# Two large writes of staged rows, moved on the ScalarE queue out of the step that ends a block

## The chip, the cores and the metric

One core of one Trainium2 chip runs the whole program. The metric is the device time of one execution in microseconds (us), as the median of the runs shown. A profiled execution of its own gives the trace; times in it are counted from the start of its span.

## The reference, cut to what matters

A long convolution (by FFT, over 12480 positions, 128 channels, batch 2) is gated by its input and goes through two dense layers:

```
h_filt = (maximum(pos_emb @ w1, 0) @ w2) * window
y = irfft(rfft(x * v, n=L) * rfft(h_filt, n=L), n=L)[:, :S]    # L = 2 * S
x = (x * y).reshape(B * S, 128)
h = x @ w_in1;  x = (h * clip(h + 3, 0, 6) / 6) @ w_out1       # 128 -> 2048 -> 128
h = maximum(x @ w_in2, 0);  out = (h * h) @ w_out2
```

## The kernel before

The program has three stages. The first (to about 64 us) makes the filter. The second, the convolution, is a loop of steps `i`, 0 to 97, written out by hand; every engine runs its instructions in the order of the program, and this order is what the change touches. The third (from about 490 us) takes 64 tiles of 390 tokens through the dense layers.

The convolution works on 32 groups of four channels, three items to a group: item 3g is the filter, 3g+1 and 3g+2 are the two batch entries. In step `i` item `i+3` gets its first transform (`s1`, TensorE line 178, eight matmuls), then `twiddle` on VectorE (lines 188 to 194, the last sum on GpSimd for filter items). Item `i+2` is rounded to a high part by ScalarE (`split1`, tile `h`, line 202); GpSimd subtracts that to make the low part (tile `l`, line 203). Item `i` gets its second transform (`s2`, line 217, twelve matmuls of which the first two need `h` and the next two `l`). Then come `filt` (ScalarE, lines 224 to 226) for a filter item, or `prod` (lines 236 to 241, VectorE and GpSimd) for a batch item. Item `z = i-2`, if it is a batch item, gets its inverse transform (`s3`, line 248) and is copied by ScalarE (`keep`, line 257) into a tile of staged rows, `stg`. So a step whose `z` is a filter item (`z % 3 == 0`, that is `i % 3 == 2`) has neither `s3` nor `keep`.

A block is four groups, twelve steps. When the last item of a block is kept, in step 12b+13 for block b, ScalarE itself issues the DMAs that write the 128 staged rows to memory: two of 4 rows (`zda`) and two of 60 rows (`zdb`, 1350 KB each), in `write`, line 360. There are two `stg` tiles, used in turn. The last block, 7, is finished apart: its large rows are written from SyncE's queue after the loop. SyncE also issues the loads of `x` and `v` (lines 149, 150), nine items ahead; GpSimd multiplies them (`product`, line 155).

Of the kernel before, what the change touches and what calls it, by code (L numbers as in the profile page):

```python
# [30 lines left out]
ZA = 4  # L31
# [8 lines left out]
def tile_hyena_moe(ctx: ExitStack, tc, xg, vg, xT, pos, w1d, w2d, win, fmat, twc,  # L40
                   tws, dcs, inv, vtab, w_in1, w_out1, w_in2, w_out2, out):
    nc = tc.nc
# [6 lines left out]
    zds = [tc.dram_tile([2, ZA, NBLK, K1, 64], F32, name="zda"),  # L49
           tc.dram_tile([2, 64 - ZA, NBLK, K1, 64], F32, name="zdb")]  # L50
# [95 lines left out]
    def load(g, b):  # L146
        xt = xv.tile([N1, 4, 128], F32, name=f"x{g}_{b}", tag="x", bufs=3)
        vt = xv.tile([N1, 4, 128], F32, name=f"v{g}_{b}", tag="v", bufs=5)
        nc.sync.dma_start(xt, xg[g, b])
        nc.sync.dma_start(vt, vg[g, b])  # L150
        us[(g, b)] = (xt, vt)

    def product(g, b):
        xt, vt = us[(g, b)]
        nc.gpsimd.tensor_tensor(vt, vt, xt, ALU.mult)
        us[(g, b)] = vt
# [11 lines left out]
    def s1(i, pool=None):  # L168
        g, s = divmod(i, 3)
        ps = bank(f"p1_{i}", pool)  # L170
        for c in range(4):
            if s == 0:
                ch = 4 * g + c
                src = hs[ch // 32][:N1, ch % 32, :]
            else:
                src = us[(g, s - 1)][:, c, :]
            o = 256 * (c % 2)
            nc.tensor.matmul(ps[:, c // 2, o:o + 2 * K1], src, fm)  # L178
        ps1s[i] = ps

    def twiddle(i):
        pv = ps1s.pop(i).rearrange("p a (s f) -> p (a s) f", s=2)[:, :, :2 * K1]
        at = vp.tile([128, 4, 2, K1], F32, name=f"a1_{i}", tag="A", bufs=3)
        bt = vp.tile([128, 4, 2, K1], F32, name=f"b1_{i}", tag="B", bufs=3)
        cw, sw = (w.rearrange("p r k -> p (r k)").unsqueeze(1)
                   .to_broadcast([128, 4, 2 * K1]) for w in (cc, ss))
        av, bv = (t.rearrange("p s r k -> p s (r k)") for t in (at, bt))
        nc.vector.tensor_tensor(bv, pv, sw, ALU.mult)  # L188

        on_pool = i and i % 3 in SUM1_POOL  # L190
        first = av if on_pool else pv
        nc.vector.tensor_tensor(first, pv, cw, ALU.mult)  # L192
        eng = nc.gpsimd if on_pool else nc.vector
        eng.tensor_tensor(at, first.rearrange("p s (r k) -> p s r k", r=2),  # L194
                          bt[:, :, ::-1, :], ALU.add)
        g1[i] = at

    def split1(i):
        gt = g1.pop(i)
        h = vp.tile([128, 4, 2, K1], F32R, name=f"h1_{i}", tag="hi", bufs=3)  # L200
        l = vp.tile([128, 4, 2, K1], F32R, name=f"l1_{i}", tag="lo", bufs=3)
        nc.scalar.activation(h, gt, AF.Copy)  # L202
        nc.gpsimd.tensor_tensor(l, gt, h.bitcast(F32), ALU.subtract)  # L203
        hi1[i], lo1[i] = h, l

    def s2(i):
        ps = bank(f"p2_{i}")
        h, l = hi1.pop(i), lo1.pop(i)
        for o in range(2):

            pv = ps[:, o, :K4].rearrange("p (s k) -> p s k", s=4)
            terms = ((o, 0), (1 - o, 1 if o == 0 else 2))
            ops = [(dcl[:, m], h[:, :, r, :]) for r, m in terms]
            ops += [(dch[:, m], l[:, :, r, :]) for r, m in terms]
            ops += [(dch[:, m], h[:, :, r, :]) for r, m in terms]
            for n, (wt, x) in enumerate(ops):
                nc.tensor.matmul(pv, wt, x, start=(n == 0), stop=(n == len(ops) - 1))  # L217
        ps2s[i] = ps

    def filt(i):  # L220
        ps = ps2s.pop(i)
        hr = vp.tile([128, K4], F32, name=f"hr_{i}", tag="hr", bufs=1)
        h2 = vp.tile([128, 2, K4], F32, name=f"hq_{i}", tag="h2", bufs=1)
        nc.scalar.activation(hr, ps[:, 0, :K4], AF.Copy)
        nc.scalar.activation(h2[:, 0], ps[:, 1, :K4], AF.Copy)
        nc.scalar.activation(h2[:, 1], ps[:, 1, :K4], AF.Copy, scale=-1.0)
        hh[i // 3] = (hr, h2)

    def prod(i):
        ps = ps2s.pop(i)  # L230
        hr, h2 = hh[i // 3]
        pv = ps[:, :, :K4]
        at = vp.tile([128, 2, K4], F32, name=f"a2_{i}", tag="Y", bufs=3)
        bt = vp.tile([128, 2, K4], F32, name=f"b2_{i}", tag="B", bufs=3)
        on_pool = i % 3 in SUM2_POOL
        nc.vector.tensor_tensor(bt, pv, h2, ALU.mult)
        first = at if on_pool else pv
        nc.vector.tensor_tensor(first, pv, hr.unsqueeze(1).to_broadcast([128, 2, K4]),
                                ALU.mult)
        eng = nc.gpsimd if on_pool else nc.vector  # L240
        eng.tensor_tensor(at, first, bt[:, ::-1, :], ALU.add)
        y2[i] = at

    def s3(i):
        y = y2.pop(i)
        ps = bank(f"p3_{i}")
        for r in range(2):
            nc.tensor.matmul(ps[:, r, :K4], iv[:, r], y[:, r])  # L248
        ps3s[i] = ps

    def keep(i):
        g, s = divmod(i, 3)
        blk, ch0 = g // 4, (g % 4) * 4
        ps = ps3s.pop(i)
        if blk not in stg:
            stg[blk] = sp.tile([128, K1, 2, 2, 16], F32, name=f"stg{blk}", tag="stg")
        nc.scalar.activation(
            stg[blk][:, :, :, s - 1, ch0:ch0 + 4].rearrange("p k r c -> p r c k"),
            ps[:, :, :K4].rearrange("p r (c k) -> p r c k", c=4), AF.Copy)
        if g % 4 == 3 and s == 2:  # L260
            sv = stg.pop(blk).rearrange("p k r b c -> p k (r b c)")
            if blk == NBLK - 1:

                for h, t in enumerate((za, zb)):
                    nc.scalar.dma_start(t.rearrange("k d r b c -> k d (r b c)")[:, blk], sv[64 * h:64 * h + 1])
                tail.append(sv)
            write(blk, 0, sv)
            if blk < NBLK - 1:
                write(blk, 1, sv)


    with tc.tile_pool(name="mlp", bufs=2, side="right") as mp, \
# [83 lines left out]
    with tc.tile_pool(name="cv_ps", bufs=4, space=PSUM) as vps:  # L356
        def write(blk, z, sv, queue=nc.scalar):
            lo, hi = ((0, ZA), (ZA, 64))[z]
            for h in range(2):
                queue.dma_start(zds[z][h, :, blk], sv[64 * h + lo:64 * h + hi])  # L360

        tail = []
        s1(0)
        twiddle(0)
        s2(1)
        s1(3)
        split1(0)
        twiddle(3)
        s2(2)
        product(1, 0)  # L370
        product(1, 1)
        load(2, 0)
        load(2, 1)
        for i in range(NI + 2):

            a, z = i + AH, i - 2
            if i < NI and i not in (1, 2):
                s2(i)
            if 3 < a < NI:
                s1(a)  # L380
            if 0 <= z < NI and z % 3:
                s3(z)
            if 2 < a - 1 < NI:
                split1(a - 1)
            if 0 <= i < NI:
                if i % 3 == 0:
                    filt(i)
                else:
                    prod(i)
            if 3 < a < NI:  # L390
                twiddle(a)
            if 0 <= z < NI and z % 3:
                keep(z)
            if i == 27:
                raw_weight(1)

            for t, f in ((a + 6, load), (a + 3, product)):
                g, s = divmod(t, 3)
                if s and (2 if f is load else 1) < g < G:
                    f(g, s - 1)  # L400
            if i == NI - 1:

                room = hp.tile([128, 2, 3, FF // 4], F32, tag="h2", name="room")
                room0 = hp.tile([128, 7, 512], F32, tag="h3", name="room0")
                other = parts[(1, 3)] = decoding(None, 1, 3, nc.gpsimd)
                for _ in range(5):
                    next(other)
                decode(None, 1, 0)
                next(other)
                next(other)  # L410
                parts[(1, 1)] = decoding(None, 1, 1)
                for _ in range(5):
                    next(parts[(1, 1)])
                za, zb = (room0[:K1, k].rearrange("k (d r b c) -> k d r b c", d=NBLK, r=2, b=2) for k in (0, 1))
                vt = {0: room0[:K1, 2, :4 * N1].rearrange("k (q r n) -> k q r n", q=2, r=2)}
                xt = {0: room0[:, 3, :TOK]}
                tile_loads(0, za, zb, vt[0], xt[0])
# [313 lines left out]
```

## Time and profile before

| | before |
|---|---|
| median of 3 runs | 2869.82 us (2868.83 to 2870.09) |
| the profiled execution's own time | 2869.38 us |
| its span in the trace | 2867.6 us |
| granted TensorE clock, mean | 0.991 of 2.4 GHz |
| TensorE busy: matmul, weight load | 2779.6 us, 2711.9 us |
| VectorE, ScalarE, GpSimd busy | 2122.8, 2006.1, 1570.8 us |

The span runs from the first instruction to the last; 1.8 us of the execution lie outside it. DMA-issuing instructions stand in the trace, on the queue of the engine that issues them (`ACTq`, `SPq`), but are not counted as busy time of the engine. Matmuls overlap each other, so that a busy TensorE is not one at its peak; the weight loads (`PEld`) show its waits more closely.

### The profile page before, as it was taken

The page shows a single profiled execution, that of the slowest core. Times are in us where ns is not written, and L with a number is a line of the kernel's source. Part 1 is how long each engine was busy: PE and PEld are TensorE (multiplying, and loading weights), DVE is VectorE, ACT ScalarE, POOL GpSimd, SP SyncE. Part 2 cuts the span into 40 slices and gives each one's busy share as a digit, 9 for nine tenths or more (in the row PEclk, how much of TensorE's full clock was granted, in tenths as well). Part 3 has the DMA queues.
Part 4 walks back from the last instruction along what each step waited for, and adds up shares of the span by engine and source line. Part 5 has one row for each costly group of instructions (what it writes and reads, how often), then busy time and mean ns, then how long its engine had stood idle before and what let it go on. Part 6 is the DMA issues. An engine that isn't in the chain of part 4 may idle for free.

```text
span 2867.6 us, 42099 instructions
## 1 busy us (share of the span) xinstructions
PE 2779.6 (97%) x15712; PEld 2711.9 (95%) x15712; DVE 2122.8 (74%) x2280; ACT 2006.1 (70%) x2630; POOL 1570.8 (55%) x1020
## 2 busy tenths in 40 slices
PE   7999998888999999999999999999999999999999
PEld 5888887778999999999999999999999999999999
DVE  6888888899877777777777777777777777777666
ACT  6445445666777777777777777777777777777776
POOL 4888885655455555555555555555555555554444
PEclk9999999999999999999999999999999999999999
DMA  4343433321011111111110111111111111110000
GB/s 158 103 137 106 140 108 88 101 60 30 24 27 26 26 26 27 26 26 26 26 27 24 26 26 27 26 26 26 26 26 26 26 26 27 26 26 6 10 12 15
DMA packets 139419, 125.77 MB, mean 44 GB/s; under 512 B 99692, under 2 KB 122702, under 8 KB 137806
## 3 DMA queue, kind: packets, MB, share of 16 engines
q1 hardware_dynamic: 128322, 89.23, 11.4%
q10 hardware_dynamic: 10892, 33.86, 4.0%
q8 instruction: 123, 2.02, 0.3%
q14 instruction: 82, 0.67, 0.1%
HBM read 86.64 MB, written 36.37 MB: 43 GB/s over the span
## 4 chain that ended last, share of the span: by engine, by line
PE 83%; DVE 7%; issue 5%; ACT 2%; POOL 2%; DMA 0%; POOLq 0%; ACTq 0%; DVEq 0%
PE acc L561 36%; PE ph L515 36%; PE p L217 4%; PE py L459 3%; PE p L178 2%; PE p L248 1%; DVE g L531 1%; ACT h L331 1%; DVE a L194 1%; POOL l L203 1%; DVE b L188 1%; DVE p L192 1%; DVE wa L106 1%; DVE wa L104 0%; DVE gl L544 0%
## 5 line engine op out<-in xcount | busy, mean ns | idle before, releaser
L544 POOL TENSOR_TENSOR gl<-g,gh 128x780 fp32r<-128x780 f32 x522 | 984.2, 1885 | 1156.1 <-ACT gh L541 1151.5
L541 ACT ACTIVATE gh<-g 128x780 fp32r<-128x780 f32 x1024 | 869.1, 849 | 111.7 <-DVE g L531 61.9
L561 PE MATMUL acc<-gh,wp 128*128 128x390 f32 x4096 | 922.4, 347 | 6.3 <-DVE wp L119 6.3
L531 DVE SCALAR_TENSOR_TENSOR g<-r,ph 128x780 f32<-128x780 f32 x512 | 494.2, 966 | 350.8 <-POOL gl L544 285.8
L561 PEld LDWEIGHTS acc<-gh,wp 128*128 128x128 f32 x4096 | 729.6, 189 | 6.6 <-issue 6.6
L534 DVE SCALAR_TENSOR_TENSOR g<-ph,r 128x780 f32<-128x780 f32 x512 | 496.4, 970 | 277.8 <-POOL gl L544 244.1
L522 ACT ACTIVATE r<-ph,three 128x780 f32<-128x780 f32 x512 | 467.5, 913 | 254.5 <-PE ph L515 239.9
L515 PE MATMUL ph<-oh,wp 128*128 128x390 f32 x2048 | 635.7, 351 | 5.5 <-DVE g L531 4.2
L515 PE MATMUL ph<-xh,wp 128*128 128x390 f32 x2048 | 618.7, 343 | 0.0
L524 ACT ACTIVATE r<-ph 128x780 f32<-128x780 f32 x512 | 422.4, 825 | 235.8 <-PE ph L515 233.8
L561 PE MATMUL acc<-gl,wp 128*128 128x390 f32 x2048 | 537.9, 344 | 21.4 <-POOL gl L544 18.9
L544 DVE TENSOR_TENSOR gl<-g,gh 128x780 fp32r<-128x780 f32 x502 | 501.2, 998 | 0.6
L561 PEld LDWEIGHTS acc<-gl,wp 128*128 128x128 f32 x2048 | 372.9, 189 | 33.2 <-POOL gl L544 23.3
L515 PEld LDWEIGHTS ph<-oh,wp 128*128 128x128 f32 x2048 | 385.4, 191 | 7.7 <-DVE g L531 6.1
L515 PEld LDWEIGHTS ph<-xh,wp 128*128 128x128 f32 x2048 | 381.4, 189 | 0.0
L515 PE MATMUL ph<-ol,wp 128*128 128x390 f32 x1024 | 350.5, 342 | 0.0
L515 PE MATMUL ph<-xl,wp 128*128 128x390 f32 x1024 | 348.4, 340 | 0.0
L202 ACT ACTIVATE h<-a 128x720 fp32r<-128x720 f32 x96 | 76.7, 806 | 221.5 <-DVE a L194 133.8
L203 POOL TENSOR_TENSOR l<-a,h 128x720 fp32r<-128x720 f32 x96 | 168.0, 1750 | 94.1 <-ACT h L202 94.1
L515 PEld LDWEIGHTS ph<-ol,wp 128*128 128x128 f32 x1024 | 194.8, 190 | 0.3 <-DVE ol L475 0.3
L515 PEld LDWEIGHTS ph<-xl,wp 128*128 128x128 f32 x1024 | 192.6, 188 | 0.0
L447 POOL TENSOR_TENSOR pn<-za,zb 90x256 f32<-90x256 f32 x126 | 132.2, 1068 | 0.0
(90 smaller groups left out, 2711.0 us busy)
## 6 DMA issues: line engine op xcount, KB each, us to landing
zdb<-stg ACTq DMA_DIRECT2D x14, 1350.0 KB
x<-xg SPq DMA_DIRECT2D x64, 196.0 KB
v<-vg SPq DMA_DIRECT2D x64, 196.0 KB
out<-ot ACTq DMA_DIRECT2D x64, 195.0 KB
xt<-xT SPq DMA_DIRECT2D x63, 195.0 KB
za<-zdb SPq DMA_DIRECT2D x60, 180.0 KB
zb<-zdb SPq DMA_DIRECT2D x60, 180.0 KB
vt<-vtab SPq DMA_DIRECT2D x63, 137.8 KB
```

What stands on the lines that cost most here:

```text
L203: nc.gpsimd.tensor_tensor(l, gt, h.bitcast(F32), ALU.subtract)
L217: nc.tensor.matmul(pv, wt, x, start=(n == 0), stop=(n == len(ops) - 1))
L447: nc.gpsimd.tensor_tensor(t[:, :, r], za[:, :, r], zb[:, :, 1 - r], op)
L459: nc.tensor.matmul(ps[:, o:o + n], pm[j][q][:, r, b, :], v[:, q, r, :n], start=(r == 0), stop=(r == 1))
L515: nc.tensor.matmul(ps[:, c, :TOK], wt, x, start=(m == 0), stop=(m == 2))
L522: nc.scalar.activation(r, ph[n][:, :, :TOK], AF.Relu, bias=three)
L524: nc.scalar.activation(r, ph[n][:, :, :TOK], AF.Relu)
L531: nc.vector.scalar_tensor_tensor(g, r, 6.0, pv, ALU.min, ALU.mult)
L534: nc.vector.scalar_tensor_tensor(g, pv, 0.0, r, ALU.max, ALU.mult)
L541: nc.scalar.activation(h, g, AF.Copy)
L544: eng.tensor_tensor(l, g, h.bitcast(F32), ALU.subtract)
L561: nc.tensor.matmul(ps, wt, x, start=(q == 0 and m == 0), stop=(q == NP - 1 and m == len(ops) - 1))
```

## The change

For blocks 0 to 6 the two writes of 60 rows no longer follow the writes of 4 rows. They go into a list, and each of the next two steps without a `keep` issues one of them from ScalarE: steps 12b+14 and 12b+17.

```
             write(blk, 0, sv)
             if blk < NBLK - 1:
-                write(blk, 1, sv)
+
+                late_rows.extend((blk, h, sv) for h in range(2))
...
-        tail = []
+        tail, late_rows = [], []
...
             if 0 <= z < NI and z % 3:
                 keep(z)
+            elif late_rows:
+                blk, h, sv = late_rows.pop(0)
+                nc.scalar.dma_start(zds[1][h, :, blk], sv[64 * h + ZA:64 * h + 64])
```

ScalarE's instructions at the end of block 2, from the last copy of the block on, before. The first number in a name is the item; `stg2` is the block's tile, and what stands in brackets is what an instruction waits for (`DMAHW` are the counters that tell of a DMA's landing).

```order
L257 ACTIVATE stg2_1741<-p3_35_2105 128x2x4x90 [waits PE_49]
L360 DMA zda_65<-stg2_1741 4x5760 [waits DMAHW3_49,Activation_49]
L360 DMA zda_65<-stg2_1741 4x5760 [waits DMAHW5_49]
L360 DMA zdb_66<-stg2_1741 60x5760 [waits DMAHW6_49]
L360 DMA zdb_66<-stg2_1741 60x5760 [waits DMAHW7_49]
L202 ACTIVATE h1_40_2150<-a1_40_2117 128x720 [waits DVE_49]
L202 ACTIVATE h1_41_2190<-a1_41_2159 128x720 [waits DVE_49,PE_49]
```

The same place now:

```order
L257 ACTIVATE stg2_1740<-p3_35_2105 128x2x4x90 [waits PE_49]
L361 DMA zda_65<-stg2_1740 4x5760 [waits DMAHW3_49,Activation_49]
L361 DMA zda_65<-stg2_1740 4x5760 [waits DMAHW5_49]
L202 ACTIVATE h1_40_2148<-a1_40_2117 128x720 [waits DVE_49]
L397 DMA zdb_66<-stg2_1740 60x5760 [waits DMAHW6_49]
L202 ACTIVATE h1_41_2189<-a1_41_2157 128x720 [waits DVE_49,PE_49]
L224 ACTIVATE hr_39_2193<-p2_39_2168 128x360 [waits PE_49]
```

The high part of item 40 has moved ahead of both writes of 60 rows; one of them stands between items 40 and 41, the other has left the place.

Three steps later on ScalarE, before:

```order
L202 ACTIVATE h1_42_2227<-a1_42_2199 128x720 [waits Pool_49]
L257 ACTIVATE stg3_2204<-p3_38_2224 128x2x4x90 [waits PE_49]
L202 ACTIVATE h1_43_2265<-a1_43_2236 128x720 [waits DVE_49,Activation_49]
L202 ACTIVATE h1_44_2305<-a1_44_2274 128x720 [waits DVE_49,PE_49,Activation_49]
L224 ACTIVATE hr_42_2309<-p2_42_2284 128x360 [waits PE_49,Activation_49]
```

The same place now:

```order
L202 ACTIVATE h1_42_2226<-a1_42_2198 128x720 [waits Pool_49]
L257 ACTIVATE stg3_2203<-p3_38_2223 128x2x4x90 [waits PE_49]
L202 ACTIVATE h1_43_2264<-a1_43_2235 128x720 [waits DVE_49,Activation_49]
L397 DMA zdb_66<-stg2_1740 60x5760 [waits DMAHW3_49]
L202 ACTIVATE h1_44_2305<-a1_44_2273 128x720 [waits DVE_49,PE_49,Activation_49]
```

The second write now stands between the high parts of items 43 and 44, where ScalarE had no DMA before. On the other four engines the order of the instructions is the same in both kernels.

## Rows read from the trace of the kernel before

**Rows 1.** The page: chain that ended last, share of the span by engine.

```profile
PE 83%; DVE 7%; issue 5%; ACT 2%; POOL 2%; DMA 0%; POOLq 0%; ACTq 0%; DVEq 0%
```

**Rows 2.** Windows, line 217 alone: stretch, length, busy (instructions), clock, DMA share, GB/s.

```profile
125.20:458.15 332.95, 181.56 (x900) 154.76 (x900) 0.98 0.43 128
198.75:235.44 36.69, 21.15 (x108) 18.30 (x109) 1.00 0.38 110
```

**Rows 3.** TensorE's timeline: start us, us, instruction, count, idle before and its end.

```profile
125.23 0.60 PE L217 MATMUL p<-h,dcl 128*128 128x360 f32 x1
...
198.77 0.46 PE L217 MATMUL p<-h,dcl 128*128 128x360 f32 x1
...
232.06 0.77 PE L217 MATMUL p<-h,dcl 128*128 128x360 f32 x2
...
235.46 0.63 PE L217 MATMUL p<-h,dcl 128*128 128x360 f32 x2
...
241.50 0.60 PE L217 MATMUL p<-h,dcl 128*128 128x360 f32 x2 [1.28 <-ACT h L202]
243.30 0.60 PE L217 MATMUL p<-l,dch 128*128 128x360 f32 x2 [1.21 <-POOL l L203]
...
247.25 0.60 PE L217 MATMUL p<-h,dcl 128*128 128x360 f32 x1
...
458.20 0.60 PE L217 MATMUL p<-h,dcl 128*128 128x360 f32 x1
```

**Rows 4.** Waits, 126 to 470 us: us in total, times, longest us.

```profile
POOL l L203 <- ACT h L202: 65.5, 49, 4.4
...
ACT h L202 <- DMA zda<-stg: 33.0, 5, 6.6
PEld p L217 <- ACT h L202: 13.4, 7, 2.1
PEld p L217 <- POOL l L203: 10.5, 7, 1.5
...
ACT h L202 <- DMA zdb<-stg: 6.9, 1, 6.9
...
ACT h L202 <- DVE b L188: 6.6, 1, 6.6
```

**Rows 5.** ScalarE's timeline around the end of block 2.

```profile
227.77 0.81 ACT L202 ACTIVATE h<-a 128x720 fp32r<-128x720 f32 x1 [4.55 <-DVE a L194]
...
229.19 0.47 ACT L226 ACTIVATE hq<-p 128x360 f32<-128x360 f32 x1
...
234.09 0.59 ACTq L360 DMA_DIRECT2D zda<-stg  x2
234.72 5.88 ACTq L360 DMA_DIRECT2D zdb<-stg  x2
240.64 1.50 ACT L202 ACTIVATE h<-a 128x720 fp32r<-128x720 f32 x2 [6.59 <-DMA zda<-stg]
```

**Rows 6.** GpSimd's timeline in the same stretch.

```profile
236.13 1.29 POOL L155 TENSOR_TENSOR v<-v,x 98x512 f32<-98x512 f32 x1
241.53 1.72 POOL L203 TENSOR_TENSOR l<-a,h 128x720 fp32r<-128x720 f32 x1 [4.11 <-ACT h L202]
```

**Rows 7.** Windows, all engines: PE, PEld, DVE, ACT, POOL busy, clock, DMA share.

```profile
188.00:195.30 7.30, 6.10 (x23) 5.48 (x24) 2.40 (x4) 3.90 (x6) 6.34 (x5) 0.77 0.96 307
241.50:247.20 5.70, 4.50 (x23) 3.88 (x24) 1.85 (x4) 3.07 (x5) 5.67 (x4) 1.00 0.90 297
238.30:250.50 12.20, 9.71 (x52) 8.15 (x51) 8.12 (x10) 6.79 (x9) 8.06 (x6) 1.00 0.87 254
```

**Rows 8.** Tile `stg`: count, duration in ns (least, median, most), first and last start.

```profile
L360 ACTq DMA_DIRECT2D zda<-stg x16: 246/301/513, 127.3 to 491.1; - x16
L360 ACTq DMA_DIRECT2D zdb<-stg x14: 2649/2913/3036, 128.1 to 446.7; - x14
...
L360 SPq DMA_DIRECT2D zdb<-stg x2: 397/432/468, 499.0 to 499.5; - x2
```

**Rows 9.** VectorE's timeline around the end of block 2.

```profile
230.17 0.91 DVE L236 TENSOR_TENSOR b<-p,hq 128x720 f32<-128x720 f32 x1 [0.89 <-PE p L217]
...
233.64 0.91 DVE L194 TENSOR_TENSOR a<-p,b 128x720 f32<-128x720 f32 x1
...
238.98 0.91 DVE L194 TENSOR_TENSOR a<-p,b 128x720 f32<-128x720 f32 x1
```

## The prediction

> **What bounds the kernel now.** I read the page's chain first: it lies on TensorE for 83% of the span [rows 1], so a change is worth what it takes out of TensorE's waits, or nothing. The change touches the convolution steps alone, so the next question is how long those take when nothing disturbs them. Line 217 runs twelve matmuls a step. Between 198.75 and 235.44 us, where no block ends, 108 of them (nine steps) take 36.69 us, or 12.23 us for three steps, at a granted clock of 1.00 [rows 2]. From 125.20 to 458.15 us, which begins just before the end of block 0 and closes just after that of block 6, 900 of them (75 steps, 25 times three) take 332.95 us [rows 2]; the first matmul of a step marks both ends [rows 3]. Undisturbed that would be 25 x 12.23 = 305.75 us. So **27.2 us** are lost there, and seven blocks end there.
>
> Where it goes is seen at the end of block 2. ScalarE issues the two small writes (0.59 us) and then the two large ones, and is held by these for 5.88 us; the next high part, of item 40, starts at 240.64, after 6.59 us in which ScalarE computes nothing [rows 5]. Its input was ready at 233.64 + 0.91 = 234.55 [rows 9]. GpSimd, which makes the low part from it, was done with its earlier work at 236.13 + 1.29 = 237.42 and stood for 4.11 us [rows 6]. TensorE ran dry for 1.28 us until the high part came and again for 1.21 us until the low part came [rows 3]. Step 41 starts at 247.25; step 38 had started at 232.06, and three undisturbed steps later is 244.29: 2.96 us lost [rows 3]. It is the same at all seven ends: ScalarE's high parts wait behind the DMA issues 5 + 1 times by name and once under VectorE's (33.0 + 6.9 + 6.6 = 46.5 us, 6.6 each), and the weight loads of line 217 wait seven times for the high and seven times for the low part, 13.4 + 10.5 = 23.9 us [rows 4].
>
> Seven times 2.96 is 20.7 us. The other 6.5 I put down to the clock: in 188.0 to 195.3, behind the end of block 1, the granted clock was 0.77 on average, between the two levels of 1.2 and 2.4 GHz, against 1.00 at the same place of block 2 (241.5 to 247.2) [rows 7]. In both TensorE had just waited; in the first it then ran slowly for a while.
>
> **The change part by part.**
>
> *Removed:* two issues of 2.65 to 3.04 us, median 2.91 [rows 8], from ahead of the high part. What is left ahead of it are the small writes, which end at 234.09 + 0.59 = 234.68, 0.13 us after the input is ready [rows 5, 9]. The high part then starts at about 234.7. GpSimd takes it up when its own queue allows, at 237.42, and needs 1.72 us: 239.14 [rows 6]. TensorE wants both at 241.50 - 1.28 = 240.22 [rows 3], 1.1 us later. So both waits go, and nothing else is late there: VectorE had finished the next sum, for item 41, at 239.89 during the stall [rows 9].
>
> *First half, one step later.* It stands between the high parts of items 40 and 41. ScalarE is free at 234.72 + 0.81 = 235.53 and is next wanted at 239.89, 4.36 us later; an issue at the median ends at 238.44, 1.45 us early, at the longest 1.32 us early. Cost nothing; the cover is ScalarE's wait for VectorE.
>
> *Second half, three steps on.* In an undisturbed group of three steps ScalarE waits 4.55 us for VectorE at this place [rows 5]. 2.91 us fit, with 1.6 to spare. Cost nothing, same cover.
>
> *Bounds of an issue alone.* The trace has no large write that is issued by itself on ScalarE. From below: the same shape took SyncE 0.40 and 0.47 us for block 7 [rows 8]; from above I take the whole pair, 5.88 us [rows 5], in case an issue lasts until something earlier has gone through. I take 2.91, the row of the same engine and tile; 0.4 gives the same time, since both hide. At 5.88 the high part is 1.3 (second half) to 1.5 us late. Queued behind it are the three copies of the filter, which end at 229.19 + 0.47 = 229.66; VectorE uses them at 230.17 [rows 5, 9], so 0.5 us of this is slack and at most 1.0 us remains. Fourteen times: 14 us given back.
>
> *The clock's 6.5 us.* From below 0 (the clock falls anyway), from above all of it. I take all: the low clock stands behind a wait that is gone.
>
> *Transfers, queues and buffers.* No bytes are added. The two large writes of a block now start 12 us apart; before, the DMA engines were at 0.87 of their time for the 12.2 us behind a block's end, against 0.38 undisturbed [rows 7, 2], so loads issued there have less in their way. SyncE, GpSimd, VectorE and TensorE keep their order. A staged tile is written again by the block after next, fourteen steps after its own block's end, and its second half leaves four steps after that end: ten steps, some 41 us, remain for the landing.
>
> Sum against the profiled execution: 2869.38 - 27.2 = 2842.2 us; the median of the runs lies 0.44 us above that execution, so **2842.6 us**. What follows step 89 is moved as a whole.
>
> **The rivals.**
>
> *A part comes back.* The issue lasts longer than the gap, or the clock falls without a wait. For it: the pair held ScalarE for 5.88 us, and nothing shows what it waited for. Against it: all fourteen lie between 2.65 and 3.04, whichever stood first [rows 8]. At the upper bound 14 us come back: 2856.6 us; with the clock's 6.5 alone 2849.1 us.
>
> *No change: transfers bind.* If the stall were the transfers' (0.87 of the engines' time), splitting them in time would gain nothing, since the bytes stay: 2869.8 us. For it: the DMA share. Against it: what TensorE waits for is a high part, which no DMA feeds, and GpSimd's only listed wait is for it too, 65.5 us [rows 4], none for a loaded tile. The Trainium skill ("DMA: Bandwidth & Descriptors", section "Issuing engines are not separate DMA queues") says that all issuing engines share the same 16 DMA engines, and that what is saved by where a DMA is initiated is the sequencer's time, usually small beside the transfer. By that rule the time would stay at 2869.8. The row disagrees on "small": 5.88 us on ScalarE's queue, with TensorE waiting behind it.
>
> *Slower: each issue holds ScalarE to the end of the traffic ahead of it.* There would then be fourteen stalls in place of seven. The place is the high part behind each write. It is covered by the gap (4.4 to 4.55 us) and by 0.5 us of slack, so it costs from an issue of about 5 us on; it eats the 27.2 us when each costs TensorE 1.94 us, at about 7 us, and is slower from there. The traffic behind a block's end lasts 12 us at 0.87 [rows 7]; an issue of 8 us would cost 14 x 3.0 = 42 us and give 2869.8 - 27.2 + 42 = 2884.6 us. Against it: 3.04 us is the longest in the trace, and in fourteen cases none lasted as long as the traffic.
>
> **How the numbers follow.** Forecast (2840 to 2847 us, some tenths of a microsecond left per block): 0.79. A part comes back (2847 to 2862): 0.12. No change: 0.05. Slower: 0.04. About 0.2%, or 5.7 us, can be told from no change. The range takes in the forecast and the greater part of the second case: 2839 to 2853 us, which leaves out less than 2 in 10. Faster: 0.79 + 0.12 = 0.91; same 0.05; slower 0.04.
>
> **What would show it.** Right: 900 matmuls of line 217 from the step behind block 0's end take 306 to 309 us; in that stretch the weight loads' waits for high and low parts are under 3 us; fourteen issues of at most 3 us, each followed by a high part that still waits for VectorE; a clock of 1.00 behind every block's end. Wrong: a high part that waits for a DMA issue, now fourteen times; GpSimd waiting for a load; a late product on VectorE behind the filter's copies; or the same 27 us turning up as a wait between step 89 and the first tile of the dense layers.

## The result and the profile after

The changed kernel takes 2842.7 us (median of 4 runs, 2840.06 to 2843.33) against 2869.32 us for the one before (4 runs beside them, 2868.39 to 2870.09): a ratio of 0.9906, 95% interval 0.9888 to 0.9923. The forecast was 2842.6 us. The profiled execution has a span of 2840.9 us where it was 2867.6.

The page's chain, share of the span by engine, against [rows 1]:

```profile
PE 89%; DVE 5%; issue 2%; ACT 2%; DMA 1%; POOL 1%; SPq 0%; ACTq 0%; POOLq 0%; DVEq 0%
```

Windows, line 217 alone, over the same 75 steps as the first of [rows 2] (stretch, length, busy and count, clock, DMA share, GB/s):

```profile
126.28:432.02 305.74, 176.30 (x900) 152.46 (x900) 1.00 0.48 134
```

The 900 matmuls take 305.74 us in place of 332.95: 27.2 us less, and as long as 75 undisturbed steps. The granted clock of the stretch is 1.00, where it was 0.98. Nothing else carries weight. The program ahead of the stretch took 1.08 us longer than in the profile before (its first matmul stood at 125.23 and stands at 126.31), though it is the same program, and what follows it took 2408.83 us instead of 2409.40: -27.2 + 1.1 - 0.6 gives the 26.7 us between the spans.

Waits of all engines from 126 to 432 us (us in total, times, longest us), against [rows 4]:

```profile
ACT h L202 <- DVE a L194: 128.5, 50, 4.6
POOL l L203 <- ACT h L202: 36.6, 50, 0.9
DVE b L236 <- PE p L217: 22.3, 25, 0.9
ACT h L202 <- POOL a L194: 21.9, 26, 0.9
PEld p L217 <- issue: 9.0, 25, 0.4
```

No high part waits for a DMA, and the weight loads' waits for high and low parts (13.4 and 10.5 us before) are not in the list. GpSimd's longest wait for a high part is 0.9 us, where it was 4.4.

ScalarE's timeline around the end of block 2, against [rows 5]:

```profile
226.16 0.59 ACTq L361 DMA_DIRECT2D zda<-stg  x2
226.81 0.80 ACT L202 ACTIVATE h<-a 128x720 fp32r<-128x720 f32 x1 [0.67 <-DVE a L194]
226.83 2.81 ACTq L397 DMA_DIRECT2D zdb<-stg  x1
232.07 0.81 ACT L202 ACTIVATE h<-a 128x720 fp32r<-128x720 f32 x1 [4.46 <-DVE a L194]
...
238.96 0.81 ACT L202 ACTIVATE h<-a 128x720 fp32r<-128x720 f32 x1 [0.61 <-DVE a L194]
238.98 0.32 ACTq L397 DMA_DIRECT2D zdb<-stg  x1
```

The high part of item 40 follows the small writes at once. The first large write is held for 2.81 us and is through at 229.64; the next high part starts at 232.07, when VectorE is ready for it. The second takes 0.32 us. Both begin 0.02 us after the high part ahead of them has begun, not when it ends.

GpSimd and TensorE at the same place, from their timelines, against [rows 6, 3]:

```profile
229.47 1.72 POOL L203 TENSOR_TENSOR l<-a,h 128x720 fp32r<-128x720 f32 x1
```

```profile
232.12 0.57 PE L217 MATMUL p<-h,dcl 128*128 128x360 f32 x2
232.53 0.50 PE L217 MATMUL p<-l,dch 128*128 128x360 f32 x2
...
236.38 0.77 PE L217 MATMUL p<-h,dcl 128*128 128x360 f32 x2
```

The low part is made at 231.19, 0.9 us before TensorE starts the step, and neither row of TensorE has a wait in brackets.

Windows behind the ends of blocks 1 and 2, all engines, at the places of [rows 7] in the program (the third is the 12.2 us behind block 2):

```profile
183.20:190.50 7.30, 7.30 (x42) 6.84 (x42) 6.21 (x8) 5.87 (x8) 5.88 (x5) 1.00 0.91 265
232.10:237.80 5.70, 5.70 (x32) 5.25 (x32) 4.82 (x6) 4.87 (x7) 4.26 (x4) 1.00 0.82 222
230.40:242.60 12.20, 12.20 (x70) 11.16 (x69) 11.05 (x14) 6.25 (x8) 10.76 (x8) 1.00 0.85 230
```

TensorE is busy throughout and the clock is 1.00 at both ends, where one was 0.77. The DMA engines are about as full behind block 2's end as before (0.85 against 0.87).

### The profile page after: what moved, and what is told of

Its sections match the earlier page's. It is cut to its first block, busy times and chain, and to the rows that moved or that the text cites. A ratio compares the mean times of both kernels' runs of the same rounds, so it can differ in the third digit from the quotient of the medians.

```text
span 2840.9 us, 42092 instructions
## 1 busy us (share of the span) xinstructions
PE 2771.1 (98%) x15712; PEld 2708.3 (95%) x15712; DVE 2122.7 (75%) x2280; ACT 2006.0 (71%) x2630; POOL 1570.6 (55%) x1020
## 3 DMA queue, kind: packets, MB, share of 16 engines
q1 hardware_dynamic: 128322, 89.23, 11.5%
## 4 chain that ended last, share of the span: by engine, by line
PE 89%; DVE 5%; issue 2%; ACT 2%; DMA 1%; POOL 1%; SPq 0%; ACTq 0%; POOLq 0%; DVEq 0%
PE acc L565 36%; PE ph L519 36%; PE p L217 7%; PE p L178 4%; PE py L463 3%; PE p L248 2%; DVE g L535 1%; DMA zdb<-stg 1%; DVE wa L106 1%; ACT h L332 1%; DVE wa L104 0%; DVE gl L548 0%; POOL gl L548 0%; ACT gh L545 0%; DVE wa L100 0%
```

## The experiments

All seven are edits of the changed kernel or of the one before. A median is that of four executions; the ratio is to executions of the kernel before beside them. "Loss" is the length of the 75 steps of line 217 (900 matmuls in all) above 305.75 us, from the same view as above, in the profiled execution. The kernel before has 27.2 and the changed one 0.0.

| kernel | median us | ratio to before, 95% interval | loss us |
|---|---|---|---|
| first half early | 2844.47 | 0.9922 (0.9907 to 0.9936) | 3.4 |
| both in the next step | 2852.05 | 0.9944 (0.9929 to 0.9959) | 8.5 |
| large first, small moved | 2842.86 | 0.9912 (0.9895 to 0.9928) | 0.1 |
| both four steps later | 2842.98 | 0.9913 (0.9899 to 0.9928) | 0.0 |
| order swapped, none moved | 2855.32 | 0.9952 (0.9937 to 0.9967) | 10.5 |
| small writes from SyncE | 2900.44 | 1.0112 (1.0095 to 1.0129) | 48.6 |
| both in the next step, weight later | 2845.11 | 0.9919 (0.9904 to 0.9933) | 2.2 |

**First half early.** One large write goes back ahead of the high part.

```
             write(blk, 0, sv)
             if blk < NBLK - 1:
-                late_rows.extend((blk, h, sv) for h in range(2))
+                nc.scalar.dma_start(zds[1][0, :, blk], sv[ZA:64])
+                late_rows.append((blk, 1, sv))
```

> The first large write of a block goes back behind the two small ones, ahead of item 40's high part; the second stays one step later. Theory (an issue is held only while two DMAs issued before it still stand in the queue; what costs is how late the high part gets): the issue is held about 2.8 us, the high part starts about 3 us late, GpSimd makes the low part from about 238.4 to 240.1 on the clock of the kernel before, and TensorE wants it at 240.2, so at most 0.3 us a block is lost: 2842 to 2845 us, and the second write, alone, is issued in about 0.3 us. Rival (each large write ahead of a high part costs half of the stall): 13.6 us of the 27.2 come back, 2856 us.

2844.47 us, as the theory had it (the profiled execution was the slowest of the four, 2849.03 us). A high part that starts 2.9 us late costs nothing at the block's end: TensorE has no wait there at any of the seven ends, and the four steps behind an end are no more than 0.02 us longer than in the changed kernel. So half of the stall is not half of the loss. The 3.4 us stand six and seven steps further on, 0.1 to 0.9 us at five of the first six blocks and 1.7 at block 3. There GpSimd's product waits 0.95 to 2.6 us for a load of `x` or `v`, which it does nowhere in this stretch of the changed kernel; why these loads land later is open. All engines behind the end of block 3 and twenty us on, then the wait between:

```profile
278.00:292.00 14.00, 14.00 (x82) 12.96 (x80) 12.61 (x16) 7.16 (x10) 11.86 (x9) 1.00 0.74 207
296.50:305.50 9.00, 8.32 (x46) 7.27 (x45) 7.37 (x9) 5.46 (x8) 5.72 (x4) 1.00 0.31 94
```

```profile
POOL v L155 <- DMA v<-vg: 2.6, 1, 2.6
```

The second issue did not come as expected: tile `stg` shows both large writes held.

```profile
L269 ACTq DMA_DIRECT2D zdb<-stg x7: 2667/2842/2843, 131.0 to 427.6; - x7
L397 ACTq DMA_DIRECT2D zdb<-stg x7: 2672/2967/2985, 133.7 to 430.8; - x7
```

I had counted the second one as alone. ScalarE issues it 0.07 us after the first is through, since the high part between them does not hold the queue (at block 6 alone 0.36 us after); so it is the fourth of one group, as before the change.

**Both in the next step.**

```
             elif late_rows:
-                blk, h, sv = late_rows.pop(0)
-                nc.scalar.dma_start(zds[1][h, :, blk], sv[64 * h + ZA:64 * h + 64])
+                for blk, h, sv in late_rows:
+                    nc.scalar.dma_start(zds[1][h, :, blk], sv[64 * h + ZA:64 * h + 64])
+                late_rows.clear()
```

> Both large writes are issued in the first step without a copy, one step after the small ones, one behind the other. Theory: they are held 2.8 and about 3.0 us, 5.8 together in a gap of about 4.4, so that the next high part is 1.4 us late; 0.5 us of that is slack, up to 1.0 us a block is lost, 7 us at most: 2843 to 2850 us. Rival (ScalarE's time does not matter once the first high part is out): 2842.7 us and every step at its undisturbed length. Rival (a stall of the old size, moved): 2869 us.

2852.05 us, 2 us outside the expectation, and for another reason than the one expected. At six of the seven ends the pair is held 5.7 to 5.9 us and hardly anything is lost (0.03 to 0.17 us a block between ends). At the end of block 1 one step takes 11.74 us in place of 4.27. ScalarE's timeline there, tile `stg` from 177 to 191 us, SyncE's load of `x`, and the waits from 176 to 196 us:

```profile
178.05 0.81 ACT L202 ACTIVATE h<-a 128x720 fp32r<-128x720 f32 x1 [0.67 <-DVE a L194]
178.08 12.94 ACTq L397 DMA_DIRECT2D zdb<-stg  x2
191.11 0.80 ACT L202 ACTIVATE h<-a 128x720 fp32r<-128x720 f32 x1 [12.25 <-DMA x<-xg]
```

```profile
L397 ACTq DMA_DIRECT2D zdb<-stg x2: 321/1564/2807, 178.1 to 190.7; - x2
```

```profile
180.78 0.32 SPq L149 DMA_DIRECT2D x<-xg  x1
```

```profile
ACT h L202 <- DMA x<-xg: 12.3, 1, 12.3
POOL l L203 <- ACT h L202: 9.3, 2, 8.3
DVE b L236 <- ACT hq L226: 8.2, 1, 8.2
...
PE p L248 <- ACT hq L226: 6.2, 1, 6.2
```

The second write is not held by its issue: the first takes 2.81 us, and the second starts 9.8 us after the first is through, at 190.7, and takes 0.32. It waits for a load of `x` to land. The DMAs of this program share a few counters that tell of their landing, and this write waits until its counter has reached a value to which the load of `x` that SyncE issued at 180.78 must add, though it needs nothing of that load. The load lands at 190.67. Everything in ScalarE's order then stands behind it, down to TensorE.

**Both in the next step, weight later.** As in the last experiment, and the 2 MB load of a weight is issued in another step:

```
-            if i == 27:
+            if i == 33:
                 raw_weight(1)
```

> Both large writes in the first step without a copy, as in the run before that cost 8 us at the end of block 1; the 2 MB load of a dense layer's weight, which stands one step after that block's end, is moved six steps later. Theory (there the second write waited 9.8 us for the landing of a load of x that shares its counter, and that load was slow because of the writes and the weight in its way): the wait shrinks by half or more and with it the loss, 2843 to 2848 us. Rival (the second write waits for the first one's transfer, the weight has no part in it): 2851 us as before.

2845.11 us, a loss of 2.2 us; block 1's end costs 0.05 us where it cost 8.1. (Of the 2.2, 1.6 stand behind block 3, where GpSimd's product waits 2.5 us for a load of `v`, as with the first half early.) The wait is gone rather than halved: moving the load also dealt the counters out anew, and the write now waits for a load that had landed. So it is shown that the wait made the loss, and not whether the weight's bytes had made the load of `x` slow.

**Large first, small moved.** At a block's end the two large writes are issued; the small ones go to the later steps.

```
-            write(blk, 0, sv)
+            if blk == NBLK - 1:
+                write(blk, 0, sv)
+            else:
+                write(blk, 1, sv)
+                late_rows.extend((blk, h, sv) for h in range(2))
...
-                nc.scalar.dma_start(zds[1][h, :, blk], sv[64 * h + ZA:64 * h + 64])
+                nc.scalar.dma_start(zds[0][h, :, blk], sv[64 * h:64 * h + ZA])
```

> At a block's end the two large writes are issued, nothing ahead of them; the two small ones follow in the steps without a copy, one each. Theory (held only behind what stands in the queue): both large writes are issued in 0.3 to 0.5 us each, no high part is late, 2842 to 2844 us, although 2.7 MB leave at once as before. Rival (an issue lasts by the size of its write, some 2.9 us for 1350 KB): ScalarE is held 5.8 us ahead of the high part, the stall is back, 2866 to 2869 us. Rival (the traffic of 2.7 MB at once costs time by itself): steps behind a block's end are longer though no high part is late.

2842.86 us, no loss, with all the bytes of the large writes leaving at once. ScalarE at the end of block 2:

```profile
227.69 0.78 ACTq L362 DMA_DIRECT2D zdb<-stg  x2
228.52 0.81 ACT L202 ACTIVATE h<-a 128x720 fp32r<-128x720 f32 x1 [0.86 <-DVE a L194]
228.54 1.53 ACTq L398 DMA_DIRECT2D zda<-stg  x1
```

The pair that held ScalarE for 5.88 us takes 0.78 with nothing ahead of it, and now it is the small write behind it, of 90 KB, that is held: 1.53 us. How long an issue lasts is not a matter of its size alone.

**Both four steps later.**

```
-            elif late_rows:
-                blk, h, sv = late_rows.pop(0)
-                nc.scalar.dma_start(zds[1][h, :, blk], sv[64 * h + ZA:64 * h + 64])
+            elif late_rows and i % 12 == 5:
+                for blk, h, sv in late_rows:
+                    nc.scalar.dma_start(zds[1][h, :, blk], sv[64 * h + ZA:64 * h + 64])
+                late_rows.clear()
```

> Both large writes are issued together, in the second step without a copy, four steps after the small ones have gone. Theory: nothing stands in ScalarE's queue then, so both take 0.3 to 0.5 us, nothing is late, 2842 to 2844 us. Rival (by size): 5.8 us in a gap of 4.55, the next high part 1.3 us late, up to 0.8 us a block lost, 2843 to 2848 us, the same as with both writes one step after the small ones.

2842.98 us, no loss. Tile `stg`: a median of 0.37 us for a large write, with one of 1.52 (the second of block 1, though ScalarE had issued nothing for 12 us before the pair).

```profile
L361 ACTq DMA_DIRECT2D zda<-stg x16: 246/274/513, 127.9 to 464.6; - x16
L397 ACTq DMA_DIRECT2D zdb<-stg x14: 321/370/1521, 140.7 to 434.6; - x14
```

**Order swapped, none moved.** The kernel before, with the large writes ahead of the small ones.

```
-            write(blk, 0, sv)
             if blk < NBLK - 1:
                 write(blk, 1, sv)
+            write(blk, 0, sv)
```

> The kernel before with its four writes at a block's end in the other order: two large, then two small, nothing moved to a later step. Theory (the first two issues of a group are free, the third and fourth each wait for one of the earlier ones): large 0.3 and 0.4 us, then about 1.5 and 2 to 2.5 us, near 5 us in all against 6.5; the high part is 4.5 to 5 us late where 6 were, its low part comes about 1 us after TensorE wants it: half of the loss or less remains, 2846 to 2856 us. Rival (bytes in the group count, not the order): 2866 to 2869 us. Rival (what holds ScalarE are the large writes alone, free when nothing stands before them): 2843 us.

2855.32 us, a loss of 10.5 us. ScalarE at the end of block 2:

```profile
230.37 0.78 ACTq L360 DMA_DIRECT2D zdb<-stg  x2
231.19 3.68 ACTq L360 DMA_DIRECT2D zda<-stg  x2
234.91 0.80 ACT L202 ACTIVATE h<-a 128x720 fp32r<-128x720 f32 x1 [4.57 <-issue]
```

Again the first two are free and the third and fourth held, now the small ones, and for less long (3.68 against 5.88 us). The group takes 4.5 us in place of 6.5 and less than half of the loss is left. At the ends themselves (the four steps behind each) it is 8.2 of the 10.5 us, 0.9 to 1.7 at each: the high part's lateness decides there, and the first 3 us of it cost nothing. The other 2.3 stand six and seven steps further on, where GpSimd's product waits 0.8 to 1.6 us for a load, as with the first half early.

**Small writes from SyncE.** At a block's end the small writes leave from the other queue; the large ones stay.

```
-            write(blk, 0, sv)
             if blk < NBLK - 1:
                 write(blk, 1, sv)
+                write(blk, 0, sv, nc.sync)
+            else:
+                write(blk, 0, sv)
```

> At a block's end ScalarE issues the two large writes and SyncE the two small ones, at the same time; nothing is moved to a later step. Theory with a queue for each engine: ScalarE's two take 0.3 to 0.4 us each, no high part is late, 2842 to 2844 us. Theory with one queue for both: the large writes can come third and fourth and are held 2 to 3 us each, up to the old stall, 2850 to 2869 us, and SyncE's loads behind them are held longer either way.

2900.44 us, slower than before. On ScalarE the theory holds: 0.32 to 0.60 us for each large write, no high part late. The stall is back by another way. SyncE's timeline behind the end of block 2, then GpSimd's and TensorE's:

```profile
241.22 0.58 SPq L362 DMA_DIRECT2D zda<-stg  x2
241.90 4.85 SPq L149 DMA_DIRECT2D x<-xg  x1
246.84 1.66 SPq L150 DMA_DIRECT2D v<-vg  x1
248.59 2.33 SPq L149 DMA_DIRECT2D x<-xg  x1
251.01 4.34 SPq L150 DMA_DIRECT2D v<-vg  x1
```

```profile
262.70 1.26 POOL L155 TENSOR_TENSOR v<-v,x 98x512 f32<-98x512 f32 x1 [7.20 <-DMA v<-vg]
263.92 1.70 POOL L203 TENSOR_TENSOR l<-a,h 128x720 fp32r<-128x720 f32 x1
```

```profile
265.67 0.97 PE L217 MATMUL p<-l,dch 128*128 128x360 f32 x2 [5.70 <-POOL l L203]
```

The loads of `x` and `v` stand behind the small writes in SyncE's order, are issued and land late, GpSimd waits for them with its product and makes the next low part only behind it. The stretch loses 48.6 us, part of it by the clock (0.95 over the stretch), and 7 more go just behind it. The expectation had the loads held longer and put no price on it.

## Why the prediction was right

*The loss and where it goes: right, to the tenth.* 27.2 us were read off as the excess over undisturbed steps, and the stretch now has the undisturbed length. That the medians also meet to a tenth (2842.6 and 2842.7) is in part luck: single executions lie between 2840.06 and 2843.33, and the 1.1 us more ahead of the stretch and 0.6 less behind it, which were not forecast, partly cancel.

*What is removed: right.* The high part of item 40 starts 0.18 us after its input (VectorE's sum ends at 226.63; forecast 0.13), the low part is ready 0.9 us before TensorE wants it (forecast 1.1). That the lateness of the high part makes the loss is shown by the runs that change how much is issued ahead of it. In the four steps behind an end, 6.5 us of issues lose 2.9 to 4.8 us, 4.5 us lose 0.9 to 1.7, and 3.5 us or 0.8 us lose nothing. The prediction's own rows give the bound: GpSimd takes the high part up 1.9 us after it could be ready (237.42 against 235.53), and the low part is 1.1 us early, so about 3.0 us of lateness are free.

*The two halves cost nothing: right; the size of an issue alone: wrong.* I took 2.91 us for both. The first, behind the small writes, is held 2.81; the second, with nothing ahead, takes 0.32, near the lower bound (0.40). Both hide. The first had 2.4 us to spare and not 1.45, because an issue starts beside the high part ahead of it, not behind it.

*The upper bound (5.88 us an issue, 14 us given back): too dear.* With the pair held 5.84 us at this place the next high part was 0.7 us late, not 1.5, and a block lost 0.17 us at most.

*The clock: right.* Line 217 of the kernel before, from one block's end to the next (the last window takes in three steps alone, 12.23 us undisturbed; the others twelve, 48.92):

```profile
125.23:178.57 53.34, 29.88 (x145) 25.61 (x145) 0.97 0.39 117
178.57:232.06 53.49, 29.06 (x144) 24.74 (x145) 0.97 0.52 155
232.06:283.94 51.88, 28.49 (x144) 24.35 (x145) 1.00 0.41 120
283.94:335.81 51.87, 28.51 (x144) 24.35 (x145) 1.00 0.41 120
335.81:389.27 53.46, 29.21 (x145) 24.91 (x145) 0.97 0.39 116
389.27:441.16 51.89, 28.50 (x144) 24.34 (x145) 1.00 0.41 120
441.16:458.20 17.04, 7.90 (x37) 6.46 (x37) 0.90 0.66 184
```

Three ends keep a clock of 1.00 and lose 2.95 to 2.97 us; four have a lower one and lose 4.42 to 4.81. What the four lose beyond 2.96 adds up to 6.5 us, and all of it came back. TensorE had waited at all seven ends, about 2.5 us each, so such a wait does not always bring the clock down; without it, it did not fall in this stretch.

*Transfers: the outcome right, one sentence wrong.* I wrote that loads behind a block's end would have less in their way. The DMA engines are about as busy there as before, 0.85 against 0.87; it just does not reach TensorE. The rival that transfers bind falls with the run that issues all the large writes at once and loses nothing. The rule weighed against it, of the Trainium skill ("DMA: Bandwidth & Descriptors", section "Issuing engines are not separate DMA queues"), that the sequencer's time is usually small beside the transfer, does hold for a write issued alone: 0.32 us, and its last bytes land 8.7 us after the issue begins (second write of block 2). The third and fourth of a group took 2.84 and 3.00 us and landed 11.5 and 14.9 us after their start (block 2 before the change). That is a fifth to a quarter of the transfer, and what it cost TensorE is what the change gave back.

*What it left out.* The text named no counter. One write of the changed kernel does wait for one: block 1's second large write is issued at 191.68, 1.6 us after the high part ahead of it has begun (190.05), and by its counter it waits for a load of `v`. It costs nothing here, since the next high part starts only at 195.40, when VectorE is ready for it. The same kind of wait cost 8 us in one experiment.

*Open.* What ends the hold of a third issue: the runs show the pattern, not the condition. A count of the issues in one queue is not enough: behind the end of block 1 in the changed kernel SyncE's load of `x` is issued in 0.32 us (180.64), but the load of `v` right behind it, only the second there, in 2.83 (181.01). And why steps ahead of the stretch differ by 1.08 us between two profiles.

## What to carry to other kernels

Measure a stall in a loop as the excess over the undisturbed step, at its own place; that excess, with its slow clock, is what can be had back. An engine that computes and also issues DMAs should issue few at a time (two from ScalarE were free here in all cases but one), in its own idle gap, with nothing urgent behind them; how they are grouped mattered more here than how large they are. Before a DMA is moved to another queue, look at what stands behind it there, and at what its landing counter makes it wait for.

## What had not been expected of the hardware

The issue of the same 1350 KB write from ScalarE takes 0.32 to 0.60 us, or 2.6 to 3.0 us behind two others. In the groups of writes at the seven blocks' ends the first two issues from ScalarE took 0.25 to 0.60 us, with one exception of 1.52 (both four steps later, block 1), and a third and fourth close behind 1.5 to 3.0 us each: two small then two large (0.25, 0.31, 2.84, 3.0), two large then two small (0.32, 0.42, 1.56, 2.07), two large then one small (0.32, 0.42, 1.53). With two writes on each of two queues at once all four were free (0.58 and 0.81 us a pair), and SyncE's next issue was held 4.85. The Trainium skill ("Perfetto Trace Analysis", section "DMA Instruction — HWDGE (DVE, Sync)") says that the profile's interval of such an instruction takes in a wait for the shared descriptor generator besides its use; a write whose time depends on what was issued before it agrees with that.
